# Attention and a two-layer block on one Trainium2 core: the first three batches in an order written as one list, V of the first batch transposed on TensorE

## The chip, the cores and the metric

The kernel runs on one core of one Trainium2 chip. A core has five engines that run beside each other and wait for one another through semaphores: TensorE (PE in the profile; its weight loads are PEld), VectorE (DVE), ScalarE (ACT), GpSimd (POOL) and SyncE (SP). Data moves between the chip's memory (HBM) and the core's SBUF by DMA, issued here by POOL (which can turn float32 into bf16 on the way) and by SP. Results of TensorE go to PSUM, eight banks of 128 x 512 float32. The metric is the device time of one launch in microseconds; several runs give a median.

## What is computed

For 8 batches of 8 heads, 576 positions and head size 64, each query sees itself and the 63 keys before it. The result is laid out as 4608 tokens of 512 features and goes through two matrix products with h - tanh(h) between them.

```python
scores = scale * np.matmul(q, k.transpose(0, 1, 3, 2))
mask = (rel >= 0) & (rel < window)          # rel = query - key, window = 64
attn = softmax(np.where(mask, scores, -1e9))
x = np.matmul(attn, v).transpose(0, 2, 1, 3).reshape(B * S, H * D)
h = x @ w_in                                # 512 -> 2048
out = (h - np.tanh(h)) @ w_out              # 2048 -> 512
```

## The kernel before

**Attention.** A batch is worked on in four pairs of heads; `g` counts the pairs through all batches (0 to 31), so batch 0 is g = 0 to 3, batch 1 is 4 to 7, batch 2 is 8 to 11. Loads put six neighbouring positions of a head in one partition. Q and K are transposed on TensorE (`tr_heads`, `tr_rows`, `tr`: groups of six or twelve small transposes into one PSUM bank) and copied to SBUF in order of position by VectorE or ScalarE (line 85 or 83, the helper `move`). There are nine query blocks of 64; a block meets a window of 128 keys. Scores come out with keys on partitions, ScalarE takes the exponential into `PT`. Keys outside the window are dealt with in one of two ways: "hide" adds a large negative number ahead of the scores by two matmuls per group (`hides`, line 276), "mask" multiplies the exponentials by 0 or 1 on VectorE (line 295). The product with V carries a column of ones, so that sums come with it; `norm` or the end of `tile_pv` takes the reciprocal and multiplies (lines 308, 310, 343).

**V.** V is needed as nine overlapping windows of 128 keys (`vw`). It is loaded eight positions to a partition, cast to `vb` (`cast_v`), sent by DMA to the even windows and one half window (`windows_v`, `keys_v`, line 150 and 165), and the odd windows are copied from the even ones on VectorE (`odd_windows`, lines 454 and 456).

**The two-layer block.** The 4608 tokens are nine chunks of 512. Attention output is transposed on TensorE (`x_tr`, line 349) or by DMA into `xT`. A hidden operation "h" is four 128x512 matmuls (line 383), a tanh on ScalarE (388) and a subtraction on VectorE (395) into `gT`; there are 16 per chunk. An output operation "y" is four matmuls (407); four of them make 128 rows of the output, which ScalarE copies to SBUF (412) and SP sends out.

**Order.** Every engine runs its instructions in the order in which the program writes them; nothing is reordered by a planner. `OPS` puts one "h" or "y" on each slot of a time line, and `at(slot, ...)` hangs attention work and loads on slots; a loop at the end walks the slots. Before the loop stands the first batch, written out, with `warm(n)`: matmuls on zeros. Chunk 0's hidden operations have slots 0 to 30, chunk 1's 32 to 62, chunk 0's outputs 64 to 79. From slot 80 on, hidden operations of chunk c and outputs of chunk c - 1 take turns. Batches 1 and 2 hang on slots 0 to 78. POOL's queue holds, in this order, the loads of batch 0, the window DMAs of batch 0, half of w_in, loads of batch 1, the other half of w_in, and later w_out and batch 3. `pace` makes POOL wait for a subtraction before it issues later loads. POOL has eight DMA semaphores in turn, so a load waits until the one eight before it has landed.

Of the kernel before, what the change touches and what calls it, by code (L numbers as in the profile page):

```python
# [7 lines left out]
F32 = mybir.dt.float32  # L8
# [7 lines left out]
def kernel(  # L16
# [62 lines left out]
    stage, rows, whole = {}, {}, {}  # L79

# [98 lines left out]
    def load_w_in(i):  # L179
        nc.gpsimd.dma_start(out=w_in_sb[i], in_=w_in_r[:, :, 1024 * i:1024 * i + 1024])  # L180
# [39 lines left out]
    nc.vector.memset(vw[0][0:64, 0], 0.0)  # L220
# [13 lines left out]

    def tr_heads(g, which, bank, eng):

        src = stage.pop((g, which))
        tp = ps[:, bank, :].bitcast(BF16)[:, 0:E * P].rearrange("c (e p) -> c e p", e=E)
        for e in range(E):
            for h in range(2):  # L240
                nc.tensor.transpose(tp[64 * h:64 * h + 64, e, :], src[:, h, D * e:D * e + D], ident[:P, :P])
        o = qs[g % 2] if which == "q" else kT[g % NK][:, 64:]
        move(eng, o.rearrange("c (p e) -> c p e", e=E), tp.rearrange("c e p -> c p e"))
# [34 lines left out]

    def tile_scores(g, grp, banks, how="hide"):

        j0, n = GROUPS[grp]
        if how == "hide":
            hides(grp, banks)
        for i in range(n):
            j = j0 + i
            for h in range(2):
                r = slice(64 * h, 64 * h + 64)
                nc.tensor.matmul(ps[:, banks[h], 64 * i:64 * i + 64], kT[g % NK][r, 64 * j:64 * j + 128],  # L288
                                 qs[g % 2][r, 64 * j:64 * j + 64], start=how == "mask", stop=how == "mask" or i == n - 1)
        o = PT[g % NPT][:, j0:j0 + n].rearrange("p j (h t) -> p h j t", h=2)  # L290
        nc.scalar.activation(o, pair_of(banks)[:, :, 0:64 * n].rearrange("p h (j t) -> p h j t", t=64),  # L291
                             ACT.Exp, scale=scale)
        if how == "mask":
            p = PT[g % NPT][:, j0:j0 + n].rearrange("p j (h t) -> p (j h) t", h=2)
            nc.vector.tensor_tensor(p, p, mask_sb.unsqueeze(1).to_broadcast([128, 2 * n, 64]), ALU.mult)

    def tile_pv(g, banks):

        b, pr = divmod(g, NP)
        for i in range(NJ + 1):  # L300
            j = min(i, NJ - 1)
            o = 65 * (i % 5)
            for h in range(2):
                nc.tensor.matmul(ps[64 * h:64 * h + 64, banks[i // 5], o:o + 65], PT[g % NPT][:, j, 64 * h:64 * h + 64],
                                 vw[b % 2][:, j, 2 * pr + h, :], start=True, stop=True)
        ov = pair_of(banks)[:, :, 0:325].rearrange("p n (i c) -> p n i c", c=D + 1)
        rc = sm_pool.tile([128, 2, 5, 1], F32, tag="rc2", name="rc2")
        nc.vector.reciprocal(rc, ov[:, :, :, D:D + 1])
        xo = xs[b % 2].rearrange("p (n i) r d -> p n i r d", i=5)
# [379 lines left out]
```

## Time and profile before

| | |
|---|---|
| median of 3 runs | 334.57 us (332.91 to 336.35) |
| profiled execution | 334.17 us, its span 332.4 us |
| TensorE, VectorE, ScalarE, POOL busy | 315.9, 199.5, 185.1, 110.5 us |
| hidden matmuls (L383) | 576, 146.8 us busy |
| output matmuls (L407) | 560, 140.8 us busy |
| subtraction (L395), tanh (L388) | 144 of 689 ns, 144 of 599 ns |
| mean granted TensorE clock | 0.984 |

"Busy" is the union of the recorded intervals of an engine. Matmuls overlap each other, so one of 379 ns occupies TensorE for about 216 ns when they follow one another (64 output matmuls with what lies between them fill 16.5 us). The page's "chain that ended last" follows the last instruction back to what released it at each step. A wait for several semaphores is put down to the one that came last.

### The profile page before, as it was taken

To read this page: it belongs to the slowest core of one execution; us is meant where nothing else is said; L and a number is where in the kernel's file an instruction comes from. 1 tells how busy PE (TensorE), PEld (TensorE's weight loads), DVE (VectorE), ACT (ScalarE), POOL (GpSimd) and SP (SyncE) were. 2 spreads that over 40 slices of the span, in tenths; PEclk is the share of its full clock that TensorE was granted. 3 is DMA by queue.
4 is the path that set the end of the run, shared out by engine and by line. 5 is a ranking of instruction groups with operands and counts; after the bars stand their busy time and mean duration, and the time that the engine had idled before them with its cause. 6 is when DMAs were issued, how large, how long until landed. Compare 5 with 4: busy or idle time off the path is not lost.

```text
span 332.4 us, 6239 instructions
## 1 busy us (share of the span) xinstructions
PE 315.9 (95%) x2435; PEld 175.3 (53%) x2435; DVE 199.5 (60%) x342; ACT 185.1 (56%) x339; POOL 110.5 (33%) x163
## 2 busy tenths in 40 slices
PE   6868999899999999999999999999999999999995
PEld 2544565555555655555555555555554444444444
DVE  4578698983257675767676666766665444334400
ACT  3545878872566666656666666555544344444411
POOL 8827597005920845434624493300000000000000
PEclk9599999999999999999999999999999999999999
DMA  8999998993796299384976968978004001000021
GB/s 159 184 173 191 212 161 120 199 190 101 123 198 125 41 163 236 81 118 116 176 133 113 180 142 140 204 126 205 32 34 104 32 34 63 32 34 32 32 97 64
DMA packets 46766, 40.68 MB, mean 122 GB/s; under 512 B 18416, under 2 KB 40048, under 8 KB 46544
## 3 DMA queue, kind: packets, MB, share of 16 engines
q0 software_dynamic: 21344, 20.06, 40.1%
q1 hardware_dynamic: 25184, 19.92, 23.6%
q8 instruction: 19, 0.31, 0.4%
q10 hardware_dynamic: 208, 0.29, 0.3%
q14 instruction: 11, 0.09, 0.1%
HBM read 36.70 MB, written 10.62 MB: 142 GB/s over the span
## 4 chain that ended last, share of the span: by engine, by line
PE 71%; DMA 9%; POOL 7%; DVE 7%; ACT 3%; issue 2%; POOLq 0%; DVEq 0%; ACTq 0%
PE ps L407 34%; PE ps L383 27%; DMA wi<-in_moe_w_in_dram 4%; PE ps L332 3%; DMA kall<-in_k_dram 3%; PE ps L316 3%; DVE xs L343 2%; PE ps L249 2%; DMA vw<-vb 2%; DVE qt L85 2%; POOL qall L96 1%; DVE gT L395 1%; POOL kall L96 1%; POOL vall L143 1%; POOL vb L85 1%
## 5 line engine op out<-in xcount | busy, mean ns | idle before, releaser
L383 PE MATMUL ps<-xT,wi 128*128 128x512 bf16 x576 | 146.8, 379 | 2.9 <-DVE gT L395 1.2
L407 PE MATMUL ps<-w_out_sb,gT 128*128 128x512 bf16 x560 | 140.8, 379 | 0.3 <-ACT ysb L412 0.3
L395 DVE TENSOR_TENSOR gT<-ps,th 128x512 bf16<-128x512 f32 x144 | 98.5, 689 | 68.6 <-ACT th L388 67.2
L388 ACT ACTIVATE th<-ps 128x512 f32<-128x512 f32 x144 | 86.0, 599 | 80.8 <-PE ps L383 77.0
L383 PEld LDWEIGHTS <-wi 128*128 128x128 bf16 x576 | 60.5, 113 | 48.1 <-issue 3.0
L407 PEld LDWEIGHTS <-gT 128*128 128x128 bf16 x560 | 52.2, 98 | 53.0 <-issue 0.8
L318 ACT ACTIVATE pt<-ps 128x384 bf16<-128x384 f32 x66 | 32.3, 489 | 24.1 <-PE ps L316 24.1
L85 POOL COPY vb<-vall 72x1024 bf16<-72x1024 bf16 x24 | 24.7, 1052 | 32.6 <-DMA vall<-in_v_dram 29.8
L343 DVE TENSOR_TENSOR xs<-ps,rc 64x576 bf16<-64x576 f32 x44 | 33.2, 755 | 1.1
L412 ACT ACTIVATE ysb<-ps 128x512 f32<-128x512 f32 x35 | 21.0, 599 | 18.9 <-PE ps L407 18.8
L85 DVE COPY qt<-ps 64x576 bf16<-64x576 bf16 x18 | 13.7, 760 | 24.1 <-ACT qt L83 24.1
L85 POOL COPY qb<-qall 96x768 bf16<-96x768 bf16 x20 | 16.6, 830 | 24.6 <-DVE pt L322 16.4
L332 PEld LDWEIGHTS <-pt 128*128 128x128 bf16 x198 | 16.5, 98 | 15.3 <-DVE pt L322 0.8
L332 PE MATMUL ps<-vw,pt 128*128 128x130 bf16 x198 | 22.0, 220 | 0.4 <-DVE pt L322 0.4
L316 PE MATMUL ps<-qt,kt 128*128 128x128 bf16 x198 | 21.8, 219 | 0.0
L316 PEld LDWEIGHTS <-kt 128*128 128x128 bf16 x198 | 15.4, 98 | 8.9 <-issue 0.3
L85 POOL COPY kb<-kall 96x768 bf16<-96x768 bf16 x20 | 16.6, 828 | 3.0 <-DMA kall<-in_k_dram 3.0
L322 DVE TENSOR_TENSOR pt<-pt,ps 128x1152 bf16<-128x1152 bf16 x22 | 16.4, 745 | 0.8 <-ACT pt L318 0.8
L83 ACT ACTIVATE kt<-ps 128x576 bf16<-128x576 bf16 x22 | 14.4, 654 | 1.6 <-PE ps L249 1.5
L291 ACT ACTIVATE pt<-ps 128x640 bf16<-128x640 f32 (+1 forms) x20 | 12.5, 648 | 2.9 <-PE ps L288 2.9
L96 POOL DMA_DIRECT2D qall<-in_q_dram x15 | 9.9, 662 | 7.9 <-DMA wi<-in_moe_w_in_dram 7.0
L83 ACT ACTIVATE qt<-ps 64x576 bf16<-64x576 bf16 x18 | 11.5, 638 | 1.0 <-PE ps L249 0.9
(79 smaller groups left out, 205.1 us busy)
## 6 DMA issues: line engine op xcount, KB each, us to landing
out_dram<-ysb SPq DMA_DIRECT2D x35, 256.0 KB
vall<-in_v_dram POOLq DMA_DIRECT2D x5, 576.0 KB, 10.7
qall<-in_q_dram POOLq DMA_DIRECT2D x4, 576.0 KB, 11.6
kall<-in_k_dram POOLq DMA_DIRECT2D x4, 576.0 KB, 11.5
kall<-in_k_dram POOLq DMA_DIRECT2D x15, 144.0 KB, 5.4
qall<-in_q_dram POOLq DMA_DIRECT2D x15, 144.0 KB, 5.2
wi<-in_moe_w_in_dram POOLq DMA_DIRECT2D x2, 1024.0 KB, 11.3
w_out_sb<-in_moe_w_out_dram POOLq DMA_DIRECT2D x2, 1024.0 KB, 14.3
```

The lines of the kernel that those rows point to most:

```text
L83: nc.scalar.activation(o, i, ACT.Copy)
L85: eng.tensor_copy(o, i)
L96: eng.dma_start(out=t, in_=(q if n == "q" else k)[b, pr::NP].rearrange("h (p e) d -> p h (e d)", e=E))
L316: nc.tensor.matmul(sp[:, i, :], kT[g % NK][:, 64 * j:64 * j + 128], qT[g % NR][:, :, 64 * j:64 * j + 64], start=True, stop=True)
L318: nc.scalar.activation(PT[g % NPT][:, 3 * grp:3 * grp + 3, :], sp, ACT.Exp, scale=scale)
L332: nc.tensor.matmul(ps[:, 5 + grp, 130 * i:130 * i + 130], PT[g % NPT][:, j, :], vw[b % 2][:, j, 2 * pr:2 * pr + 2, :], start=True, stop=True)
L343: nc.vector.tensor_tensor(xo[r, :, :, pr, :], ov[r, :, :, h, 0:D], rc[r].to_broadcast([64, 3, 3, 64]), ALU.mult)
L383: nc.tensor.matmul(hp, w_in_tile(ki, m), chunk_tile(c)[:, :, ki % 2, 64 * (ki // 2):64 * (ki // 2) + 64], start=(ki == 0), stop=(ki == 3))
L388: nc.scalar.activation(th, hp, ACT.Tanh)
L395: nc.vector.tensor_tensor(gT[c][:, m, :], hp, th, ALU.subtract)
L407: nc.tensor.matmul(yp, gT[c][:, m, s * 128:(s + 1) * 128], w_out_sb[:, m, :], start=(m == 0), stop=(m == M - 1))
L412: nc.scalar.activation(ysb, ps[:, yp_bank(c, s), :], ACT.Copy)
```

## The change

The order of everything up to slot 80 is now one list, `FIRST`. Each entry is an operation, its pair or chunk, and where it matters the engine: T is a transposing group of q, k or v and C the copy that follows it; H, S, E and M are hide, scores, exponential and mask of the first five (a) or last four (b) query blocks; W transposes V back and X copies it into the windows; PV and N are the product with V and the normalisation; Y and Z transpose x and copy it; h, t and u are hidden matmuls, tanh and subtraction; y and yo are outputs; kc, qc and Vc are casts; mv is the window DMAs and next loads of a batch; od is the odd windows. `BANKS` gives each its PSUM bank, two banks of a pair always next to each other.

Batch 0's V is loaded like q and k (six positions to a partition), transposed on TensorE into `vT` (in order of position), and transposed back in windows of 128 keys, from which copies fill all nine windows: no window DMA and no odd-window copy for batch 0. Its scratch space is the second `gT` buffer. Both weights are loaded straight after batch 0, ahead of batch 1. Chunk 0's 16 hidden operations come first, then its outputs with the attention of batch 1, then chunk 1's hidden operations with batch 2. Hides are used for pairs 0 to 3 and 7, masks for the other pairs up to 11. The `warm` calls after the first nine matmuls are gone. Slots from 80 on are as before, but for a step or two of batch 3, one turn of x, and a fourth output buffer.

```diff
+    scratch = g_pool.tile([128, M, TOK], BF16, tag="gT", name="scratch").rearrange("p m t -> p (m t)")
+    v0 = scratch[0:P, 0:H * E * D].rearrange("p (h c) -> p h c", h=H)
+    vT = scratch[:, H * E * D:H * E * D + NP * (64 + S)].rearrange("p (i c) -> p i c", i=NP)
...
+    def load_v0(pr):
+        nc.gpsimd.dma_start(out=v0[:, pr::NP], in_=v[0, pr::NP].rearrange("h (p e) d -> p h (e d)", e=E))
+        stage[pr, "v"] = v0[:, pr::NP]
...
-    for pr in range(NP):
-        load_v(0, pr)
+    load_v0(0)
     make_ident()
     load(1, "k", G)
     load(1, "q", G)
     make_hide()
+    load_v0(1)
+    load(2, "k", G)
+    load(2, "q", G)
+    load_v0(2)
+    load_v0(3)
+    load(3, "k", G)
+    load(3, "q", G)
     make_seen()
...
+    load_w_in(0, 0, 512)
+    load_w_in(0, 512, 1024)
+    load_w_in(1)
+    load_w_out(0)
+    load_w_out(1)
+    for pr in range(NP):
+        load_v(1, pr)
+    for g in 4, 5:
+        load(g, "k", G)
+        load(g, "q", G)
...
+    FIRST = """
+        Ha.0 Ha.1 qc.0.D Tq.0 kc.0.A Tv.0 Tk.0 Tk.1 Cq.0.D Tq.1 Cv.0.A Ck.0.D Wb.0 Cq.1.D Sa.0 Ck.1.A Ea.0 Tv.1
+        Sa.1 Hb.0 Ea.1 Wa.0 Xb.0.D Sb.0 Cv.1.D Wb.1 Xa.0.D Tk.2 Eb.0 Xb.1.D Ck.2.A Tq.2 PV.0 N.0 Hb.1 Cq.2.A
+        Wa.1 Sb.1 Tv.2 Eb.1 Tv.3 Hb.2 Sb.2 Xa.1.D Cv.3.D Ha.2 Sa.2 Cv.2.A Eb.2 Tk.3 Tq.3 Wa.2 Ea.2 Wb.2 Ck.3.D
+        Cq.3.A Wb.3 Wa.3 Xa.2.D Xb.2.A Ha.3 Sa.3 Ea.3 Xb.3.D Xa.3.D PV.2 Hb.3 Sb.3 PV.1 Eb.3 N.2 N.1 PV.3 Yb.0.0
+        Zb.0.0.A N.3 Ya.0.0 Ya.0.1 Za.0.0.D Yb.0.1 Za.0.1.A Zb.0.1.D h.0.0 h.0.1 h.0.2 t.0.0 t.0.1 u.0.0 h.0.3
+        h.0.4 t.0.2 h.0.5 t.0.3 h.0.6 u.0.1 u.0.2 u.0.3 t.0.4 h.0.7 t.0.5 u.0.4 h.0.8 h.0.9 t.0.6 u.0.5 t.0.7
+        u.0.6 h.0.10 u.0.7 t.0.8 t.0.9 u.0.8 h.0.11 t.0.10 u.0.9 t.0.11 u.0.10 u.0.11 h.0.12 t.0.12 h.0.13
+        u.0.12 t.0.13 h.0.14 u.0.13 t.0.14 h.0.15 Vc.4.A y.0 t.0.15 u.0.14 Vc.6.A y.1 u.0.15 kc.4.D Vc.7.D y.2
+        y.3 qc.4.D Vc.5.A y.4 mv.1 yo.0 kc.5.D Tk.4 Tq.4 y.5 Ck.4.A Tk.5 qc.5.A Cq.4.D Sa.4 Tq.5 Cq.5.D Ck.5.A
+        Ea.4 y.6 Ma.4 Sb.5 Sb.4 Sa.5 y.7 kc.6.D Eb.5 Eb.4 Mb.5 Ea.5 y.8 qc.6.A od.1 kc.7.A Tk.6 y.9 Tq.6 qc.7.D
+        Ck.6.A Ma.5 Mb.4 y.10 Cq.6.A Tq.7 yo.1 Cq.7.D Tk.7 Sa.6 Sb.6 Ck.7.A y.11 PV.4 Vc.9.D Ea.6 PV.5 y.12
+        Vc.10.D yo.2 y.13 Ma.6 N.4 Eb.6 kc.8.A Mb.6 Hb.7 Ha.7 Tk.8 N.5 Vc.8.D qc.8.D Sa.7 Ck.8.D Sb.7 PV.6
+        Vc.11.A mv.2 Ea.7 Eb.7 N.6 y.14 kc.9.A Yb.1.0 PV.7 qc.9.D Zb.1.0.A Tq.8 Tq.9 y.15 Cq.8.A N.7 Cq.9.D
+        Yb.1.1 yo.3 Ya.1.0 Tk.9 Ya.1.1 Za.1.0.D Sa.8 Zb.1.1.A Ck.9.A Sb.8 Za.1.1.D h.1.0 Ea.8 qc.10.D h.1.1 od.2
+        Sb.9 Eb.8 h.1.2 t.1.0 Eb.9 t.1.1 kc.10.D t.1.2 Mb.8 Tq.10 Ma.8 Sa.9 u.1.0 Cq.10.A PV.8 u.1.1 Ea.9 h.1.3
+        u.1.2 t.1.3 Tk.10 Ck.10.A h.1.4 Mb.9 Ma.9 h.1.5 Sa.10 t.1.4 u.1.3 N.8 kc.11.D PV.9 Ea.10 u.1.4 N.9 h.1.6
+        t.1.5 Tk.11 t.1.6 h.1.7 u.1.5 u.1.6 qc.11.A t.1.7 Ma.10 u.1.7 h.1.8 t.1.8 Ya.2.0 Tq.11 Sb.10 Eb.10 Mb.10
+        Cq.11.A h.1.9 Ck.11.A h.1.10 Za.2.0.D t.1.9 u.1.8 PV.10 t.1.10 N.10 Sb.11 h.1.11 Sa.11 u.1.9 u.1.10
+        Eb.11 Yb.2.0 Ea.11 Mb.11 Ma.11 h.1.12 h.1.13 t.1.11 Zb.2.0.A PV.11 t.1.12 u.1.11 N.11 u.1.12 h.1.14
+        h.1.15 t.1.13 t.1.14 t.1.15 u.1.13 Ya.2.1 Za.2.1.D Yb.2.1 Zb.2.1.A u.1.14 u.1.15
+    """.split()
...
+    def v_tr(c, g):
+        j0, n = half(c)
+        tp = v_psum(c, g)
+        for i in range(n):
+            nc.tensor.transpose(tp[:, i].rearrange("p h d -> p (h d)"), vT[:, g, 64 * (j0 + i):64 * (j0 + i) + 128], ident)
+
+    def v_copy(c, g, eng):
+        j0, n = half(c)
+        move(eng, vw[0][:, j0:j0 + n, 2 * g:2 * g + 2, 0:D], v_psum(c, g))
...
+    def first_moves(b):
+        even_windows(b, G, Y, G, Y, G)
+        if b == 1:
+            for g in 6, 7:
+                load(g, "k", G)
+                load(g, "q", G)
+            for pr in range(NP):
+                load_v(2, pr)
+            for g in 8, 9:
+                load(g, "k", G)
+                load(g, "q", G)
+        else:
+            for g in 10, 11:
+                load(g, "k", G)
+                load(g, "q", G)
...
+    warm(9)
+    for t in FIRST:
+        if t == "y.0":
+            see()
+            copy_mask()
+        first(t)
+    load_all(3, "q")
+    load_all(3, "k")
+    load_v_all(3)
+    at(67, lambda: nc.gpsimd.tensor_copy(tick, gT[1][0:1, 9, 0:1]))
...
-    STEPS = {2: (0, 0, 49, 57), 3: (72, 79, 86, 93), 4: (100, 107, 114, 121), 5: (128, 135, 142, 149)}
-    TURNS = {13: (97, 3, 99, 3), 15: (110, 4, 111, 3)}
+    STEPS = {3: (74, 80, 87, 93), 4: (100, 107, 114, 121), 5: (128, 135, 142, 149)}
+    TURNS = {13: (98, 3, 99, 3), 15: (110, 4, 111, 3)}
```

## The prediction

> **What bounds the kernel now.** I read the page's shares and slices first, then the chain of work that ended last, then a table of stretches.
>
> ```profile
> span 332.4 us, 6239 instructions
> ...
> PE 315.9 (95%) x2435; PEld 175.3 (53%) x2435; DVE 199.5 (60%) x342; ACT 185.1 (56%) x339; POOL 110.5 (33%) x163
> ...
> PE   6868999899999999999999999999999999999995
> ...
> PEclk9599999999999999999999999999999999999999
> ...
> PE 71%; DMA 9%; POOL 7%; DVE 7%; ACT 3%; issue 2%; POOLq 0%; DVEq 0%; ACTq 0%
> ```
>
> TensorE is the bound, with 16.5 us of the span not busy (332.4 - 315.9). The first slices are the weak ones, in activity and in clock. The table of stretches (columns: stretch, length, busy us of PE, PEld, DVE, ACT, POOL with their instructions, clock, DMA share, GB/s) says where:
>
> ```profile
> 0.00:25.10 25.10, 17.49 (x289) 10.52 (x289) 14.97 (x36) 11.41 (x19) 15.98 (x31) 0.80 1.01 172
> 25.10:50.60 25.50, 23.89 (x293) 14.01 (x294) 21.16 (x42) 18.24 (x33) 19.30 (x27) 1.00 1.13 183
> 50.60:73.00 22.40, 20.55 (x220) 12.15 (x218) 20.05 (x40) 19.63 (x38) 5.99 (x10) 1.00 1.05 175
> 73.00:89.49 16.49, 16.49 (x120) 8.94 (x118) 5.98 (x11) 5.99 (x12) 11.34 (x18) 1.00 0.59 113
> ...
> 130.00:332.40 202.40, 197.76 (x1217) 106.53 (x1215) 111.41 (x176) 103.61 (x188) 41.64 (x58) 1.00 0.46 99
> ```
>
> Up to 25.1 us the first batch's attention runs before any chunk exists. Then come 48 us in which hidden matmuls, attention of two batches, tanh and subtractions share the core: TensorE is free for 3.5 us (47.9 - 44.44), but VectorE is busy for 41.2 of them. From 73 us the chunk-0 outputs run with VectorE at 36%. The first hidden matmul of chunk 2, where the two orders meet again, starts at 89.49. All that follows takes 332.4 - 89.5 = 242.9 us. So the change is decided ahead of 89.5 us.
>
> In single microseconds (same columns) the clock:
>
> ```profile
> 8.00:9.00 1.00, 0.99 (x17) 0.37 (x10) 0.68 (x2) 0.70 (x1) 1.00 (x2) 0.50 1.28 187
> ...
> 12.00:13.00 1.00, 1.00 (x30) 0.88 (x30) 0.34 (x1) 0.00 (x0) 0.88 (x3) 0.50 1.06 192
> ...
> 16.00:17.00 1.00, 1.00 (x8) 0.43 (x4) 0.91 (x2) 1.00 (x3) 1.00 (x2) 0.50 0.83 131
> ...
> 19.00:20.00 1.00, 1.00 (x63) 0.99 (x64) 0.45 (x2) 0.00 (x0) 0.00 (x0) 1.00 0.99 147
> ```
>
> It is half from 8.0 to 18.2 us, and TensorE is busy for most of it.
>
> **What the Trainium skill says.** "TensorE: Matmul & The Clock Gate", Part 1: the clock is set by activity windows of 3413 ns. The trace agrees: 18.2 - 8.0 = 10.2 us is three of them. The same page, Part 4: transposes do not count as busy in the way that matmuls do. The trace agrees: from 11.4 to 14.8 us TensorE did 2.1 us of transposes and about 0.7 of matmuls and stayed at half; from 14.8 to 18.2, with 2.9 us of score, hide and warm matmuls, it came up. "VectorE: DVE Perf Modes", Why PSUM operands drop a tier: a PSUM source may still be packed as 16-bit data, no more. Here a contiguous 128x512 copy takes 0.42 us and a strided 128x576 one 0.76: so I bound the new copies with these two.
>
> **The change, part by part.**
>
> *First batch, V on TensorE.* Removed: four value casts on VectorE (4 x 0.43), nine window DMAs and two odd-window copies (0.86 + 0.70). Added: four groups of 12 transposes (L241's: 0.69 us each at half clock, 0.30 at full), four more copies out of PSUM (0.76 on VectorE, 0.65 on ScalarE), 36 transposes back (nine x-transposes take 0.50 at full, so about 1.0 per pair at half), eight copies into the windows. These write 64-element runs; per 576 elements 0.47 (contiguous row) to 0.84 (strided row plus a tenth), taken 0.64. Hides for pairs 1 and 2 replace two masks: +1.12 us each on TensorE at half clock, -0.91 each on VectorE. The sum for TensorE from the first transpose to the last x-transpose at half clock: 12 x 0.69 + 4 x 1.0 + 3 x 1.12 + 4 x 0.66 (scores) + 4 x 0.7 (PV, half-clock value between 0.4 and 0.9, its 80 take 1.65 at full) + 1.0 = 22.1; at full 11.8. Before, the same sum without the 4 groups, the way back and two hides is 13.1. Half clock runs from 8.0 to 18.2. Four groups fit ahead of 8.0; 19.3 half-clock us remain; 9.5 of them are done by 18.2 (pair 1's data lands by then, 0.7 us of waiting); the other 9.8 become 4.9 at full: 23.1, if the clock comes up at 18.2. VectorE's sum here is 14.5 us from 5.2 on and its last items are three normalisations (1.04 each) in a row, then x-copies: the last of them starts behind PV of pair 3 near 23, ends near 24.5, transposes 0.25, copy 0.6. **First hidden matmul at 25.4 us against 25.1.** What the window DMAs cost comes back as TensorE work at half clock.
>
> *Weights first.* The view of waits has the wait that this removes:
>
> ```profile
> POOL qall L96 <- DMA wi<-in_moe_w_in_dram: 7.0, 1, 7.0
> ```
>
> The hidden weights land at 25.07 in the kernel before, so moving them alone gains nothing beyond 25.1. Behind them on POOL's queue now stand w_out (2 x 1024 KB), v of batch 1, then q and k. By GB/s times length the queue moves 4.3 MB by 25.1 and 172-183 GB/s after. Ahead of w_out's end lie 6.3 MB (about 36 us), batch 1's v 6.9 (39), q/k of pairs 4 and 5 7.5 (42). They are wanted at 39 to 44: hidden, with 0 to 1 us to spare; a microsecond late costs one.
>
> *Chunk 0 alone, then its outputs with batch 1.* 16 hidden operations x 4 x 0.216 = 13.8 us; ScalarE 16 x 0.60 and VectorE 16 x 0.69 fit under it. 25.4 + 13.8 = 39.2. Outputs: 16 x 0.864 = 13.8, with six pairs' transposes (0.50), five scores (0.45), one hide (0.7), four PV (0.44), x-transposes (1.0): 22.5 us on TensorE; ScalarE 21.6, VectorE 18.6. The even windows' DMAs and the loads of pairs 6 and 7 are issued only after V's casts, near 43.3; three issues of 0.62 and 4-5 us to landing (5.2-5.4 is the page's median) put k of pair 6 at 49-50, and VectorE, in order, stands at its cast from 47.7. The masks behind it wait, TensorE at pair 6's transposes. I take 1.5 us, between 0 and 3. End: 63.2.
>
> *Chunk 1 with batch 2.* TensorE 18.9 us; VectorE 16 x 0.685 + 4 x 1.04 + 8 masks 3.6 + odd windows 1.4 + copies and casts 1.9 = 22.1: VectorE is the bound. The odd windows wait for DMAs issued after the last cast, near 59.5, and landing near 65.5, where VectorE is ready at 63.8: 1.7 (0 to 3). Subtractions queue behind, tanh's three buffers fill, TensorE stands. Last, pair 12's transposes and first scores stand ahead of chunk 2's first hidden matmul with nothing between: two ScalarE copies behind the last tanh and x-copy, 1.6 us (1 to 3). 63.2 + 22.1 + 1.7 + 1.6 = **88.6 us, against 89.5.** Deferred past this point: a score group and pair 13's q transposes (0.17 + 0.26) and their bubbles, 0.7.
>
> *The rest*: 242.9 + 0.7. The moved turns (97 to 98) and steps cost nothing: hidden and output matmuls on both sides cover them; without that cover 0.3 each. A fourth output buffer: nothing, since the view of waits after 89 us names none on these buffers. On SP's queue the window DMAs of batch 2 now stand behind three outputs of chunk 0, whose evictions are done by 57: nothing, and what the outputs are late if not. Batch 3's loads leave POOL near 62, not 53.7; their 1.8 MB land by 74, and pair 12's first transposes need them at 86: nothing, with 12 us of cover, and microsecond for microsecond beyond. Span 88.6 + 243.6 = 332.2, against 332.4. The profiled execution took 334.17, 1.77 beyond its span; the median shown, 334.57, is 0.4 above that. 332.2 + 1.77 is 333.97; I forecast **334.0**, no change.
>
> **The rivals.**
> *The order fits as written* (faster). For it: VectorE is at 36% from 73 to 89 us, and the new order gives that stretch attention work. TensorE's work from 25 to the meeting point is 13.8 + 22.5 + 18.9 = 55.2 us where the kernel before spends 64.4. If the clock is up earlier (h0 at 23.4, -2.0), the loads arrive in time (-1.5, -1.7) and the end costs 0.6 (-1.0), it is 327.8. Against it: VectorE's 22.1 in the last stretch.
> *The clock stays at half* (slower). Place: the window from 14.8 to 18.2, where the new order has about 2.0 us of real matmuls, not 2.9, among transposes; the warm matmuls at 17.7, 20.4 and 22.2 are gone. If it stays half at 18.2, the next window is nearly all transposes, and first-batch work ends 2.0 us later (27.4 for h0); the wait for normalisation then leaves the window to 28.4 half idle, so hidden matmuls run at 0.43 until 31.9: half of 4.5, 2.2 more. 334.0 + 4.2 = 338.2. It decides if the clock is still 0.5 after 21.6.
> *Batch 1 behind the weights is late* (slower): its v lands at 44, not 39; ScalarE's casts of it stand ahead of chunk 0's last tanh, so subtraction and outputs wait: +5, 339.0. Against: the DMA share of 1.0-1.1 held through 73 us.
>
> **How the numbers follow.** No change 0.43, fits 0.25, half clock 0.22, late loads 0.10. Within 1% (331.2 to 337.9, about what a measurement of this kernel can tell from no change) falls most of the first and a third of the others' nearer ends. Faster by over 1%: 0.22 of the second plus 0.05 of the first; slower: 0.15 + 0.09 + 0.06. The 8-in-10 range runs from 327.8 to 339.5; the likeliest case alone runs from 330.5 to 337.
>
> **What would show it.** First hidden matmul at 25 to 26 us; clock half to 18.2 (or beyond 21.6, the second rival); VectorE over 90% busy in the last stretch ahead of chunk 2, its waits on DMA at a k cast near 48 and at the odd windows near 64; chunk 2's first hidden matmul at 88 to 89; all after it within 1 us of 243. I am wrong if chunk 2 starts by 84, if h0 begins before 24, or if the stretch after 89 changes by over 1 us.

## The result, and the profile after

| | before | after |
|---|---|---|
| median (lowest to highest, runs) | 334.57 us (332.91 to 336.35, 3) | 344.74 us (344.13 to 345.02, 3) |
| profiled execution, its span | 334.17, 332.4 us | 345.02, 343.3 us |
| first hidden matmul | 25.1 us | 23.2 us |
| first hidden matmul of chunk 2 | 89.5 us | 98.7 us |

The changed kernel is slower: the ratio is 1.0299, interval 1.0212 to 1.0387. The forecast was 334.0 us, range 327.8 to 339.5. It was wrong. Ratios here and below leave out executions over 1.5% longer than the shortest of their kernel, so that a ratio need not be the quotient of two medians.

The page of the changed kernel (shares, then TensorE's activity and clock in 40 slices of 8.6 us, then the chain that ended last):

```profile
span 343.3 us, 6496 instructions
...
PE 320.9 (93%) x2554; PEld 178.4 (52%) x2554; DVE 200.2 (58%) x346; ACT 191.7 (56%) x342; POOL 102.9 (30%) x155
...
PE   8879949939979999999999999999999999999996
...
PEclk9999996987989999999999999999999999999999
...
PE 70%; DMA 11%; POOL 6%; DVE 6%; ACT 3%; issue 3%; POOLq 0%; DVEq 0%
```

The span is 10.9 us longer. TensorE is busy for 5.0 of them (320.9 against 315.9) and idle for 5.9 more (22.4 against 16.5). The front, slices 1 and 2, is full in clock in this profile. Two holes have come, slice 6 (43 to 51 us) and slice 9 (69 to 77 us), and the clock dips in or behind each.

The same kernel by the stages that the prediction used (stretch, length, busy us of PE, PEld, DVE, ACT, POOL, clock, DMA share, GB/s):

```profile
0.00:23.19 23.19, 18.28 (x376) 12.39 (x377) 14.57 (x36) 12.24 (x20) 15.03 (x29) 1.00 1.08 184
23.19:37.19 14.00, 14.00 (x68) 7.29 (x66) 10.14 (x16) 9.51 (x17) 1.90 (x3) 1.00 1.12 208
37.19:67.77 30.58, 25.58 (x331) 15.11 (x329) 16.98 (x37) 20.03 (x33) 14.62 (x23) 0.89 0.82 133
67.77:98.69 30.92, 23.64 (x261) 13.19 (x256) 21.05 (x41) 19.34 (x36) 9.37 (x14) 0.89 0.58 91
98.69:343.30 244.61, 239.37 (x1534) 130.42 (x1531) 137.44 (x217) 130.62 (x239) 61.95 (x88) 0.99 0.53 106
```

Against the forecast: front 23.2 (25.4), -2.2; chunk 0's hidden operations 14.0 (13.8), +0.2; outputs with batch 1 30.6 (24.0), +6.6; chunk 1 with batch 2 30.9 (25.4), +5.5; the rest 244.6 (243.6), +1.0. That is +11.1, the whole distance between 343.3 and the forecast span of 332.2. Both bad stages have TensorE idle (5.0 and 7.3 us) and a clock of 0.89.

The view of waits of the changed kernel from 25 to 100 us (who waited, for whom: us in total, times, longest):

```profile
POOL tick L653 <- DVE gT L355: 20.9, 1, 20.9
...
POOL vw L173 <- PE ps L541: 7.7, 1, 7.7
DVE kb L93 <- DMA kall<-in_k_dram: 6.6, 1, 6.6
DVE qb L93 <- DMA qall<-in_q_dram: 6.2, 2, 5.7
...
POOL vw L173 <- ACT vb L91: 5.4, 1, 5.4
PE ps L511 <- DVE kb L93: 5.0, 1, 5.0
...
PE ps L511 <- DVE qb L93: 3.3, 1, 3.3
```

It is the same chain twice: POOL waits ahead of the window DMAs (`vw`), a cast on VectorE waits for a load that stands behind them, TensorE waits for the cast ahead of its transposes. (The second wait of POOL is put down to scores, L541; in the list, `mv.2` follows a V cast that is itself behind exponentials on ScalarE.) POOL's own time line shows the first of them (start, length, what, and in brackets the idle time ahead of it):

```profile
40.68 0.61 POOL L173 DMA_DIRECT2D vw<-vb  x1 [5.37 <-ACT vb L91]
41.28 1.06 POOL L158 DMA_DIRECT2D vw<-vb  x2
42.33 0.66 POOL L104 DMA_DIRECT2D kall<-in_k_dram  x1
```

For 5.4 us POOL stands for ScalarE's last V cast, with pair 6's k, which depends on no cast, behind it. That k is issued at 42.33; VectorE gets it at 51.76, 9.4 us later. In stretches of 2 us (columns as above):

```profile
40.00:42.00 2.00, 2.00 (x20) 1.18 (x19) 0.35 (x2) 1.02 (x3) 1.32 (x3) 1.00 0.11 20
42.00:44.00 2.00, 2.00 (x33) 1.27 (x30) 0.76 (x1) 2.00 (x4) 2.00 (x4) 1.00 1.04 107
50.00:52.00 2.00, 0.00 (x0) 0.00 (x0) 0.24 (x1) 0.00 (x0) 0.67 (x1) 0.74 1.21 206
52.00:54.00 2.00, 1.83 (x10) 1.00 (x11) 1.85 (x4) 1.50 (x2) 1.69 (x2) 0.50 0.98 152
...
72.00:74.00 2.00, 0.00 (x0) 0.00 (x0) 0.26 (x1) 0.00 (x0) 0.00 (x0) 1.00 1.26 230
...
76.00:78.00 2.00, 1.27 (x22) 0.92 (x23) 2.00 (x5) 0.00 (x0) 0.00 (x0) 0.50 1.31 203
```

The DMA engines are all but idle up to 42 (share 0.11), while POOL stands; then all at once they have more than they can do, at 107 GB/s with the windows among it. TensorE is idle from 47 to 52 and from 71 to 74, and with each hole comes a spell of half clock of 6.8 us, from 51.0 to 57.8 and from 74.8 to 81.7. In the second, q of pair 10 is issued at 65.44 behind the windows of batch 2 and used at 73.74.

### The profile page after: what moved, and what is told of

The parts are those of the page before. It is cut to its first block, busy times and chain, and to the rows that moved or that the text cites. A ratio compares the mean times of both kernels' runs of the same rounds, so it can differ in the third digit from the quotient of the medians.

```text
span 343.3 us, 6496 instructions
## 1 busy us (share of the span) xinstructions
PE 320.9 (93%) x2554; PEld 178.4 (52%) x2554; DVE 200.2 (58%) x346; ACT 191.7 (56%) x342; POOL 102.9 (30%) x155
## 4 chain that ended last, share of the span: by engine, by line
PE 70%; DMA 11%; POOL 6%; DVE 6%; ACT 3%; issue 3%; POOLq 0%; DVEq 0%
PE ps L338 30%; PE ps L367 29%; DMA vall<-in_v_dram 5%; DMA kall<-in_k_dram 3%; DMA qall<-in_q_dram 2%; PE ps L288 2%; DVE xs L299 2%; PE ps L276 2%; POOL vb L93 2%; DMA scratch<-in_v_dram 1%; POOL vw L158 1%; PE ps L251 1%; PE ps L563 1%; DVE qt L93 1%; PE ps L382 1%
## 5 line engine op out<-in xcount | busy, mean ns | idle before, releaser
L367 PE MATMUL ps<-w_out_sb,gT 128*128 128x512 bf16 x560 | 143.2, 384 | 0.0
L278 ACT ACTIVATE pt<-ps 128x384 bf16<-128x384 f32 x60 | 29.3, 488 | 21.2 <-PE ps L276 21.1
L299 DVE TENSOR_TENSOR xs<-ps,rc 64x576 bf16<-64x576 f32 x40 | 30.2, 755 | 1.0
L93 POOL COPY vb<-vall 72x1024 bf16<-72x1024 bf16 x20 | 20.7, 1051 | 31.5 <-DMA vall<-in_v_dram 17.5
L93 DVE COPY qt<-ps 64x576 bf16<-64x576 bf16 x16 | 12.2, 760 | 22.3 <-ACT qt L91 22.3
L288 PEld LDWEIGHTS <-pt 128*128 128x128 bf16 x180 | 15.1, 98 | 13.8
L276 PE MATMUL ps<-qt,kt 128*128 128x128 bf16 x180 | 19.8, 219 | 0.9 <-DVE qt L93 0.9
L288 PE MATMUL ps<-vw,pt 128*128 128x130 bf16 x180 | 20.1, 220 | 0.0
L546 ACT ACTIVATE pt<-ps 128x640 bf16<-128x640 f32 (+1 forms) x24 | 15.2, 654 | 5.5 <-PE ps L541 5.1
L91 ACT ACTIVATE kt<-ps 128x576 bf16<-128x576 bf16 x25 | 16.3, 650 | 2.4 <-PE ps L511 2.1
L282 DVE TENSOR_TENSOR pt<-pt,ps 128x1152 bf16<-128x1152 bf16 x20 | 14.9, 743 | 0.0
L104 POOL DMA_DIRECT2D kall<-in_k_dram x15 | 9.9, 663 | 7.2 <-DMA w_out_sb<-in_moe_w_out_dram 4.3
```

What stands on the lines that cost most here:

```text
L91: nc.scalar.activation(o, i, ACT.Copy)
L93: eng.tensor_copy(o, i)
L104: eng.dma_start(out=t, in_=(q if n == "q" else k)[b, pr::NP].rearrange("h (p e) d -> p h (e d)", e=E))
L276: nc.tensor.matmul(sp[:, i, :], kT[g % NK][:, 64 * j:64 * j + 128], qT[g % NR][:, :, 64 * j:64 * j + 64], start=True, stop=True)
L278: nc.scalar.activation(PT[g % NPT][:, 3 * grp:3 * grp + 3, :], sp, ACT.Exp, scale=scale)
L288: nc.tensor.matmul(ps[:, 5 + grp, 130 * i:130 * i + 130], PT[g % NPT][:, j, :], vw[b % 2][:, j, 2 * pr:2 * pr + 2, :], start=True, stop=True)
```

## The experiments

The theory: **the place in POOL's queue.** Loads 6, 7, 10 and 11 are late because they stand behind window DMAs that wait for V's casts, and each hole then costs a spell of half clock on top. The first rival: **bandwidth.** The weights ahead of batch 1 fill the DMA engines, and the loads would be late from any place. The second: the whole order costs more than the old one, whatever its loads do.

**The loads ahead of the windows**

```diff
     def first_moves(b):
+        for g in (6, 7) if b == 1 else (10, 11):
+            load(g, "k", G)
+            load(g, "q", G)
         even_windows(b, G, Y, G, Y, G)
         if b == 1:
-            for g in 6, 7:
...
-        else:
-            for g in 10, 11:
```

> Edit: POOL issues the q and k loads of pairs 6, 7 (and of 10, 11) ahead of the window DMAs of their batch, not behind them. Queue theory: the loads stand behind window DMAs that wait for the last V cast, the DMA engines idle from 40 to 42 us meanwhile, and VectorE and TensorE then wait 5.0 and 3.3 us for k of pair 6 and q of pair 10 and drop to half clock after it. Then both stalls go with their half clock, about 4.5 + 2.5 + 3 + 2.5: 331 to 334 us, first hidden matmul of chunk 2 near 87 to 90. Bandwidth rival (weights first push everything behind them back, so that the DMA engines are simply full): the loads land no earlier, 343 to 346 us.

335.69 us (333.78 to 338.93, 7 runs), ratio 1.0033 [0.9995, 1.0072]: 9 us of the loss of 10.2 are gone by moving eight loads. Its stages 3, 4 and 5, from a profile of the longest of the seven executions (338.93 us):

```profile
38.12:64.56 26.44, 24.41 (x331) 14.41 (x329) 16.96 (x37) 19.68 (x33) 14.63 (x23) 0.94 1.06 173
64.56:89.18 24.62, 21.20 (x262) 12.59 (x257) 20.51 (x41) 19.24 (x36) 7.45 (x11) 1.00 0.58 90
89.18:337.20 248.02, 239.60 (x1534) 130.85 (x1531) 138.06 (x217) 130.96 (x239) 62.28 (x88) 0.99 0.53 105
```

Chunk 2 starts at 89.2, where the forecast had 88.6, and stages 3 and 4 take 26.4 and 24.6 where it had 24.0 and 25.4. So the order is as good as forecast, and bandwidth is not what holds it: the same bytes move. But the rest takes 248.0; its reason is looked for further down.

**The holes filled with matmuls on zeros**

```diff
     for t in FIRST:
+        if t == "Tk.6":
+            warm(20, 3)
+        if t == "Tq.10":
+            warm(14, 7)
```

> Edit: 20 matmuls on zeros ahead of pair 6's k transposes and 14 ahead of pair 10's q transposes, in the two gaps where TensorE waits; everything else as in the changed kernel. Theory that half clock after a gap is a cost of its own: clock 1.0 through both stretches, gaps as before, 339 to 341 us. If the half clock is hidden under the waits of other engines: 343 to 346 us.

340.87 us (339.66 to 342.32, 4 runs), ratio 1.0201 [1.0159, 1.0242]. Here the loads come as late as in the changed kernel, and TensorE does useless work while it waits. Stages 3 and 4:

```profile
36.96:64.25 27.29, 27.24 (x351) 15.62 (x349) 16.96 (x37) 19.90 (x33) 14.65 (x24) 1.00 0.94 152
64.25:92.77 28.52, 24.41 (x276) 13.98 (x270) 20.59 (x41) 19.35 (x36) 9.53 (x14) 0.99 0.63 99
```

The clock is 1.00 and 0.99 instead of 0.89 twice. So 3.9 of the 10.2 us (344.74 - 340.87) are the half clock behind the holes, and not the holes. Between the two profiled spans it is 5.3 us (343.3 and 338.0). Had the prediction known their length, it would still have missed this.

**w_out behind batch 1's values and pairs 4 and 5**

```diff
     load_w_in(1)
-    load_w_out(0)
-    load_w_out(1)
...
         load(g, "q", G)
+    load_w_out(0)
+    load_w_out(1)
```

> Edit: w_out is loaded behind batch 1's v and the q, k of pairs 4 and 5, not ahead of them; w_in stays first. Queue theory: batch 1's casts were not late, the gap at pair 6 stays; w_out lands near 42 and chunk 0's outputs wait for it at 37: 345 to 350 us. Bandwidth rival: the first loads of batch 1 land 10 us earlier and the stretch of batch 1 gets shorter, 335 to 342 us.

343.28 us (342.9 to 343.8, 4 runs), ratio 1.0271 [1.0234, 1.0308]: 1.5 us less than the changed kernel, and a miss of both theories. POOL's time line:

```profile
41.74 0.62 POOL L173 DMA_DIRECT2D vw<-vb  x1 [12.15 <-ACT vb L91]
```

Batch 1's values are in early, but their casts stand behind chunk 0's tanhs on ScalarE as before, and POOL now stands 12.2 us for them. K of pair 6, issued at 43.40, is used at 52.17, against 51.76 in the changed kernel. TensorE's wait there is shorter (1.7 against 5.0 us) since the outputs have already waited 2.5 us for w_out, and the hole at q of pair 10 stays at 3.5. Values that land early gain little while POOL waits for their casts. On bandwidth this run says nothing: `w_out`, for which TensorE waits until 42.6 here, still stands ahead of that load on POOL's queue.

**The loads first, but as late as before.** This parts the issue time from the place in the queue: a small GpSimd copy makes the loads of pairs 6 and 7 wait for the cast for which the windows waited. Those of pairs 10 and 11 stay where they were, and so does the second hole.

```diff
+        if b == 1:
+            nc.gpsimd.tensor_copy(tick, vb[0:1, 0, 2, 0:1])
+            for g in 6, 7:
+                load(g, "k", G)
+                load(g, "q", G)
         even_windows(b, G, Y, G, Y, G)
```

> The changed kernel, with the loads of pairs 6 and 7 ahead of batch 1's window transfers, but behind a GpSimd copy that waits for the same last V cast on ScalarE: the loads go out at the same time as the windows did, 40.7, no earlier. Rival first: if the position behind the window transfers in the queue is what made them late, they land 2 us after issue at 44 to 46, the gap at pair 6 is under 1 us and the time 338 to 340.5. If the late issue (GpSimd stands 5.4 us for ScalarE's cast) is what counts, they land at 46 to 48, 3 us of the gap stay and the time is 342 to 344.

343.16 us (342.51 to 343.32, 4 runs), ratio 1.0234 [1.018, 1.0289]. It takes both to explain. VectorE's time line in this kernel:

```profile
45.73 0.35 DVE L93 COPY kb<-kall 96x768 bf16<-96x768 bf16 x1
...
52.19 0.70 DVE L413 COPY vw<-vw 64x2080 bf16<-64x2080 bf16 x1 [5.33 <-DMA vw<-vb]
```

Issued at 41.3 and ahead of the windows, k of pair 6 is there by 45.7, 4.4 us later instead of 9.4: the place alone is worth 5 us for that load. But the windows, issued 3 us later than in the changed kernel, are now what VectorE waits for, at the odd-window copies, which start at 52.19, against 52.48 in the changed kernel. Pair 7's q cast is behind them, and TensorE stands 4.0 us. One of the two is late as long as both leave POOL after 40.7; in the first experiment the loads left from 36.2 on, while POOL would have stood idle. **What counts for batch 1 is that the loads leave while POOL would else stand and the DMA engines are all but idle; reordering what leaves after that changed mainly which of VectorE's steps waits.**

**The rest: the tick, and one step of batch 3.** In the experiment with the loads ahead, POOL's longest single wait, and the wait of TensorE for POOL's casts behind it, from 85 to 125 us:

```profile
POOL tick L649 <- DVE gT L355: 17.3, 1, 17.3
...
PE ps L251 <- POOL qb L93: 3.0, 2, 2.2
```

The changed kernel has a copy on POOL (`at(67, ...)`, L653 there; L649 here) that waits for chunk 1's tenth subtraction; batch 3's casts and batch 4's loads stand behind it. TensorE's 2.2 us, up to 116.6, are followed by half clock from 117.3 to 120.7. Without the copy (and with the loads ahead):

```diff
-    at(67, lambda: nc.gpsimd.tensor_copy(tick, gT[1][0:1, 9, 0:1]))
```

> Edit: as e1_loads_ahead, and POOL no longer waits for chunk 1's tenth subtraction (slot 67) before it casts batch 3. Theory that this wait holds batch 3 back once the stretch ahead is shorter (POOL stood 17.3 us there in e1, then batch 4's v was issued at 93.6 and landed at 111.8, and TensorE waited 2.2 us at 116.6): POOL's casts start near 72 to 75, the part after chunk 2's first hidden matmul falls from 248 back to 243 to 245: 330 to 333 us. If POOL's casts beside the last stretch slow VectorE, or batch 4's v does not come earlier: 335 to 338 us.

Ratio 0.9904 [0.9876, 0.9933] (median 334.35 of 20 runs, 329.16 to 339.56). The last stage of its profile:

```profile
86.84:330.40 243.56, 239.03 (x1533) 130.63 (x1531) 137.51 (x217) 130.51 (x239) 58.90 (x83) 0.99 0.54 105
```

TensorE's wait for POOL is gone, and the rest falls from 248.0 to 243.6, the forecast's own figure. But the 248.0 is from the longest of seven executions, and the ratio rests on the 8 shortest of 20. By the medians of all runs, each against the kernel before beside it (335.69 and 334.33; 334.35 and 334.86), leaving out the tick gains 1.9 us, and this kernel is no faster than the kernel before. And with batch 3's first step one slot later besides:

```diff
-    STEPS = {3: (74, 80, 87, 93), 4: (100, 107, 114, 121), 5: (128, 135, 142, 149)}
+    STEPS = {3: (75, 80, 87, 93), 4: (100, 107, 114, 121), 5: (128, 135, 142, 149)}
```

> Edit: as e5_no_tick, and the steps of pair 12 hang one slot later (75 instead of 74), so that chunk 2's first hidden matmul stands ahead of pair 12's first scores. Theory that the tail before chunk 2 is a wait of TensorE for the copies of pair 12 alone (1.0 us of it named so): 1 to 2 us less than e5. If the hidden matmul itself is held by the last x copies: the same as e5 within 0.5 us.

331.79 us (331.38 to 332.25, 4 runs), ratio 0.99 [0.9865, 0.9934]: 1% faster than the kernel before. The 12 runs of this kernel and of the two below that are built on it lie between 329.0 and 333.2. What the step is worth by itself isn't shown, since why the kernel without it spreads over 10 us isn't known. Stages 3 to 5:

```profile
37.78:62.73 24.95, 22.94 (x331) 13.79 (x329) 16.92 (x37) 19.69 (x33) 14.43 (x23) 1.00 1.11 182
62.73:86.33 23.60, 20.89 (x257) 12.34 (x254) 19.74 (x40) 18.40 (x35) 9.12 (x13) 1.00 0.70 104
86.33:329.90 243.57, 238.28 (x1538) 130.28 (x1534) 138.26 (x218) 130.95 (x241) 60.42 (x86) 1.00 0.53 106
```

The clock is full in all three. The second rival of the experiments has fallen: the new order, fed in time, is the shorter one, by about 1%.

**What is left of the holes.** In that kernel VectorE still stands up to 3.2 us at the odd windows and TensorE 2.0 us behind it. Two more edits on top of it:

```diff
-        Ea.4 y.6 Ma.4 Sb.5 Sb.4 Sa.5 y.7 kc.6.D Eb.5 Eb.4 Mb.5 Ea.5 y.8 qc.6.A od.1 kc.7.A Tk.6 y.9 Tq.6 qc.7.D
-        Ck.6.A Ma.5 Mb.4 y.10 Cq.6.A Tq.7 yo.1 Cq.7.D Tk.7 Sa.6 Sb.6 Ck.7.A y.11 PV.4 Vc.9.D Ea.6 PV.5 y.12
+        Ea.4 y.6 Ma.4 Sb.5 Sb.4 Sa.5 y.7 kc.6.D Eb.5 Eb.4 Mb.5 Ea.5 y.8 qc.6.A kc.7.A Tk.6 y.9 Tq.6 qc.7.D
+        Ck.6.A Ma.5 Mb.4 od.1 y.10 Cq.6.A Tq.7 yo.1 Cq.7.D Tk.7 Sa.6 Sb.6 Ck.7.A y.11 PV.4 Vc.9.D Ea.6 PV.5 y.12
...
-        Yb.1.1 yo.3 Ya.1.0 Tk.9 Ya.1.1 Za.1.0.D Sa.8 Zb.1.1.A Ck.9.A Sb.8 Za.1.1.D h.1.0 Ea.8 qc.10.D h.1.1 od.2
-        Sb.9 Eb.8 h.1.2 t.1.0 Eb.9 t.1.1 kc.10.D t.1.2 Mb.8 Tq.10 Ma.8 Sa.9 u.1.0 Cq.10.A PV.8 u.1.1 Ea.9 h.1.3
+        Yb.1.1 yo.3 Ya.1.0 Tk.9 Ya.1.1 Za.1.0.D Sa.8 Zb.1.1.A Ck.9.A Sb.8 Za.1.1.D h.1.0 Ea.8 qc.10.D h.1.1
+        Sb.9 Eb.8 h.1.2 t.1.0 Eb.9 t.1.1 kc.10.D t.1.2 Mb.8 Tq.10 Ma.8 od.2 Sa.9 u.1.0 Cq.10.A PV.8 u.1.1 Ea.9 h.1.3
```

> The changed kernel with loads 6, 7, 10, 11 ahead of the windows, without the tick at step 67, first step of batch 3 at 75, and besides with VectorE's copies from the odd windows moved back: batch 1's behind pair 7's query cast and the masks of pairs 5 and 4, batch 2's behind pair 8's second mask. Theory (VectorE standing 3.16 us at those copies is what leaves TensorE 1.95 us idle at pair 7's transposes): that gap goes under 0.8 us, chunk 2 starts at 84.5 to 85.6 instead of 86.3, 329.5 to 331.2 us. Rival (the copies are short of nothing but their windows, and PV of batch 1 then waits for them in their new place): the gap only moves, 331.5 to 333.

330.85 us (329.0 to 332.71, 4 runs), ratio 0.9871 [0.9798, 0.9943]. The four runs span what both sides expected. By the profile the rival is right: chunk 2 starts at 87.1 and not at 84.5 to 85.6, and TensorE's longest wait is now

```profile
PE ps L563 <- DVE vw L415: 2.1, 1, 2.1
```

at the product with V of pair 8, which needs those very copies. The hole has moved, and this kernel can't be told from the one without the edit. Then pair 12's transposes in other banks:

```diff
-            at(a, tr, g, "q", 2 if g < 13 else 3, A, V)
-            at(a + 2, tr, g, "k", 3, A)
+            at(a, tr, g, "q", 5 if g < 13 else 3, A, V)
+            at(a + 2, tr, g, "k", 1 if g < 13 else 3, A)
```

> The kernel with the odd windows' copies moved back, and besides pair 12's transposes into banks 5 and 1 instead of 2 and 3. Theory (the 1.0 us before chunk 2 comes from chunk 1's last subtractions alone, which hold the banks): the wait stays if it is the hidden matmuls' own (they wait for gT), so no more than 0.5 us, 329 to 331 us. Rival (pair 12's transposes wait behind the banks and hold TensorE's queue): 1 us or more less than without.

331.84 us (330.99 to 333.18, 4 runs), ratio 0.9892 [0.9827, 0.9957]. The waits at L251 that it aims at (1.2 us in all) are gone from the view, so they were waits for the banks, but the wait for the odd windows at pair 8 is 3.4 us here instead of 2.1, and the time is the same.

**Parts of the change, apart.** The kernel before, with both weights moved to just behind batch 0's windows, and nothing else:

```diff
     load_w_in(0)
+    load_w_in(1)
+    load_w_out(0)
+    load_w_out(1)
     for pr in range(NP):
         load_v(1, pr)
...
-    load_w_in(1)
...
-    at(23, load_w_out, 0)
-    at(23, load_w_out, 1)
```

> Edit: the kernel before with both weights loaded straight after batch 0's window DMAs, ahead of batch 1; its order of work is kept. Theory that weights first costs only where attention of batch 1 is wanted early: batch 1's q and k land near 40 instead of 30 to 38, its steps among chunk 0's hidden operations stand, 340 to 346 us. If the loads have slack there: 333 to 336 us.

347.9 us (347.26 to 349.95, 4 runs), ratio 1.0391 [1.0343, 1.0438]. Batch 1's values are late: VectorE stands 14.7 us at a cast, subtractions are behind it, hidden matmuls stop for 13.7. The old order mixes chunk 0 with batch 1, so the weights alone, put first, cost it 13 us; its first hidden matmul is at 24.0. The other part the other way round: the changed kernel, with batch 0's V cast and cut into windows by DMA, on SP.

```diff
-    load_v0(0)
+    load_v(0, 0)
...
-        elif n in ("Ck", "Cq", "Cv"):
+        elif n == "Cv":
+            cast_v(0, a[0], eng)
+        elif n in ("Ck", "Cq"):
...
+    FIRST = [t for t in FIRST if t[:2] not in ("Tv", "Wa", "Wb", "Xa", "Xb") and t not in ("PV.0", "N.0")]
+    i = FIRST.index("PV.2")
+    FIRST[i:i] = ["od.0", "PV.0", "N.0"]
+    FIRST.insert(FIRST.index("Cv.2.A") + 1, "w0.0")
+    FIRST_OPS["w0"] = lambda _: even_windows(0, Y, Y, Y, Y, Y)
```

> The changed kernel, but batch 0's V is taken the old way: V is cast and the windows are cut by transfers from SBUF to SBUF, with copies for the odd ones; the two sets of transposes of V and their copies are left out; everything behind the first hidden matmul as in the changed kernel. If V on TensorE is what brought the first hidden matmul from 25.1 to 23.2: it comes at 25 or later here, with TensorE at half clock in front, 345.5 to 349 us. If it gains nothing by itself: first hidden matmul at 22 to 23.5, 343.5 to 345 us.

360.99 us (358.91 to 362.56, 4 runs), ratio 1.0766 [1.0696, 1.0836], far beyond what either side expected; the first hidden matmul comes at 40.9, behind half clock from 12.0 on. TensorE's waits of this kernel:

```profile
PE ps L563 <- DVE vw L415: 11.3, 1, 11.3
PE ps L563 <- DMA vw<-vb: 4.1, 1, 4.1
```

and its DMA queues from 14.8 to 32 us (packets, megabytes, the time of the packets as a share of 16 engines):

```profile
q0 software_dynamic: 1708, 3.25, 100.4%
q1 hardware_dynamic: 648, 0.60, 13.0%
```

Five window DMAs of 0.6 MB in all leave SP between 14.9 and 18.2, beside 3.2 MB of weights and loads, and the odd-window copies that need them start at 31.9. So in the changed kernel V on TensorE is worth 16 us (360.99 - 344.74) against windows that are issued into the weights. Against windows ahead of the weights it wasn't tried, nor in the old order alone; in the kernel just above, the windows stood ahead of the weights on POOL's queue, and the front was no later than 24.0.

**What keeps the clock up in front.** Half clock from 8.0 to 18.2 was the prediction's first step, and the profile after shows none. Leaving out the hides of pairs 1 and 2 in the changed kernel:

```diff
-    HIDE = (0, 1, 2, 3, 7)
+    HIDE = (0, 3, 7)
...
+        if t in ("Ha.1", "Hb.1", "Ha.2", "Hb.2"):
+            continue
```

> Edit: the hides of pairs 1 and 2 are left out, and nothing takes their place, so keys outside the window count in these two pairs: it shows what eight plain matmuls in the first batch do to the clock and the time. Theory that hides keep the clock at full there: TensorE at 0.5 from 8 to 18 us as in the kernel before, first hidden matmul near 25 to 27 us. If the clock was up for another reason: clock 1.0, first hidden matmul at 22.5 to 23.2.

345.06 us (one run); the clock is 1.00 up to the first hidden matmul at 22.0, with TensorE busy for 16.9 us of 22. So it isn't the hides of these two pairs. Then the kernel before, with 13 warm matmuls in place of 9:

```diff
-    warm(9)
+    warm(13)
```

> Edit: the kernel before with 13 instead of 9 warm matmuls on zeros at the start, which fill TensorE's gap from 5.15 to 6.3 us and nothing else. Theory that the gaps from 4.6 to 8.0 us (TensorE busy about 45 per cent) turned the clock to half from 8 to 18 us, and that filling them is what kept it at full in the changed kernel: clock 1.0 from 8 us on, the first hidden matmul still near 25 because its weights land at 25.07: 332.5 to 334.5 us. If hides and transposes of the changed order kept it up: half clock as before, 334 to 335 us.

335.42 us (333.18 to 337.9, 12 runs), ratio 1.002 [0.9992, 1.0048], not the 332.5 to 334.5 expected. The clock holds past 8 us and falls at 13.6, after the next idle place (TensorE 1.61 us busy from 11 to 14). Last, both idle places filled, once with `idle_tr(n)`, n transposes of the identity into a bank that nobody reads, once with matmuls on zeros:

```diff
     warm(9)
+    idle_tr(18)
...
+    idle_tr(24)
     tr_heads(2, "k", 2, V)
```

> The kernel before, with transposes of the identity into a bank that nobody reads, in the two places where TensorE stands in front: 18 behind the nine warm matmuls, 24 ahead of pair 2's transposes (which wait for their load). Theory A (any work of TensorE keeps the clock up, transposes too): full clock to 17 us at least, and half for less than 4 us in front. Theory B (transposes do not count, as the prediction assumed): clock half from about 8, as in the kernel before, 334 to 337 us. Under A the time is 333 to 335.5, since the weights land at 24 to 25 in any case.

334.84 us (332.92 to 336.95, 20 runs), ratio 1.0008 [0.9986, 1.003]. Stretches of its front; the first line is the same stretch of the kernel before:

```profile
5.00:8.00 3.00, 1.45 (x37) 0.97 (x36) 1.74 (x4) 1.49 (x2) 2.86 (x8) 0.99 1.23 184
...
5.00:8.00 3.00, 2.87 (x46) 2.09 (x44) 1.32 (x3) 1.31 (x2) 2.86 (x8) 1.00 1.24 193
...
11.00:14.00 3.00, 2.17 (x62) 1.81 (x61) 1.37 (x3) 1.52 (x4) 2.50 (x4) 1.00 1.13 201
14.00:16.00 2.00, 1.24 (x43) 1.01 (x44) 1.52 (x3) 1.58 (x3) 0.86 (x2) 1.00 0.92 216
16.00:19.00 3.00, 1.76 (x26) 1.12 (x26) 1.61 (x4) 1.84 (x3) 2.49 (x4) 0.54 1.09 184
```

```diff
-    warm(9)
+    warm(13)
...
+    warm(7)
     tr_heads(2, "k", 2, V)
```

> The same two places filled with matmuls on zeros instead: 13 in front, 7 more ahead of pair 2's transposes. Both theories: full clock to 17 us at least; first hidden matmul at 23.5 to 24.5, 333 to 335.5 us. Only if the clock still falls near 14, as it did with the first place alone filled, is it something else than TensorE's idle time that brings it down.

335.0 us (332.38 to 337.1, 12 runs), ratio 1.0019 [0.9989, 1.0049]. The same stretches of this kernel, where the two differ most:

```profile
11.00:14.00 3.00, 2.63 (x59) 1.62 (x58) 1.29 (x3) 1.35 (x4) 2.64 (x5) 1.00 1.18 227
...
16.00:19.00 3.00, 1.85 (x70) 1.48 (x71) 2.35 (x5) 1.80 (x4) 2.33 (x4) 1.00 1.10 198
```

With transposes the clock stays full past 8 and past 14 and falls only at 16.2, after 3 us in which TensorE twice waited for a load; it is half until 23.0, for longer than the 4 us expected. **Transposes keep a full clock up**, as matmuls do. The Trainium skill ("TensorE: Matmul & The Clock Gate", Part 4) has it that the full clock doesn't engage for transposes, since they don't count as busy in the same way; for holding a clock that is already full these runs say otherwise. With matmuls it never falls, the first hidden matmul comes at 23.4 instead of 25.1, and the profiled span is 330.6 instead of 332.4; yet that profile is of the shortest of the 12 runs, and their median is no better than before.

Transposes count for raising the clock, too. The kernel with pair 12's transposes in other banks keeps the changed kernel's order in front, and its profile has a spell of half clock there. Here are the stretch ahead of the spell, the spell, and the spell for L581 alone, the transposes of x:

```profile
17.48:20.90 3.42, 1.85 (x66) 1.34 (x65) 2.13 (x5) 1.30 (x2) 0.85 (x2) 1.00 1.14 213
20.90:24.31 3.41, 3.05 (x26) 2.37 (x26) 1.81 (x5) 1.36 (x3) 0.00 (x0) 0.50 1.11 216
...
20.90:24.31 3.41, 2.29 (x18) 0.50 1.11 216
```

Of TensorE's 3.05 us of work in the spell 2.29 were transposes, and at its end the clock was full again. Three other profiles show the same, with 2.06 to 2.28 us of transposes in 3.15 to 3.24 of work. So the prediction read too much into the profile before, where TensorE stayed at half from 11.4 to 14.8 us with 2.1 us of transposes. It was busy for 2.64 us there, and with 13 warm matmuls it stayed at half through 2.67 us in 3.42 (from 16.96) without a single transpose.

One profile of a front is also only one case of it. Of the eight other runs that keep the changed kernel's order in front, six have a spell of half clock of 3.4 us between 11.5 and 25.2 us, and two have none; their first hidden matmul comes at 21.9 to 24.0. The kernel before, in the 31 executions taken beside the last two experiments, has a mean clock of 0.974 to 1.0; the profile that the prediction rests on has 0.984. The 11 of them at 0.995 or more have a median of 334.38 us, the other 20 of 334.70. So a full clock goes with some 0.3 us less in that kernel, which fits with filling its idle places gaining nothing that these runs can tell. With transposes the lowest mean clock of 20 runs is 0.985, with matmuls of 12 runs 0.985.

## Why the prediction was wrong

*Front* (25.4, measured 23.2). Wrong to the good side. The step was "half clock runs from 8.0 to 18.2", taken over from the profile before. There the clock fell after a stretch with 1.45 us of work in 3 (5 to 8 us); the new order has 2.9 there, of hides and of transposes, V's among them, which the prediction had set down as not counting. The added TensorE work was counted at half clock and ran at full, or nearly so: at most 3.4 us of half clock stand in front in the other runs of this order. The profile before was one case of a clock that changes from one execution to the next.

*Chunk 0 alone* (13.8, measured 14.0): right. *The rest* (243.6, measured 244.6): 1.0 us more, with a third spell of half clock in it, 3.4 us from 98.7, behind a stretch of 3.42 us in which TensorE worked for 1.30; at full clock throughout, the mended kernel (loads ahead, no tick, the step at 75) takes 243.57. The tick at slot 67 wasn't priced. What it costs here isn't shown; in the kernel with the loads ahead it is 1.9 us by the medians and 4.4 by two profiles (248.0 against 243.6).

*Outputs with batch 1* (22.5 + 1.5). This is **the step that failed**: the wait for the loads of pair 6, put at 1.5 us, and the half clock behind it, put at nothing. The mechanism was named: loads 6 and 7 behind windows behind V's casts, VectorE in order at pair 6's k, TensorE at its transposes. Its sizes were not: k usable at 51.8, not 49 to 50 (9.4 us from issue to use, where the page before has a median of 5.2 to 5.4 to landing); VectorE at its cast at 45.2, not 47.7, since the faster front brings everything forward except what waits for POOL; a wait of 6.6 us, not 1.5. So the gain in front came to nothing here.

*The price of a hole* was left out: the stall was put in as its own length. TensorE ran at half clock from 51.0 to 57.8 us, with 5.6 us of work, so by estimate 2.8 us more. The Trainium skill's page "TensorE: Matmul & The Clock Gate", in "Why this matters for your kernels", has the rule that applies: no idle gaps of TensorE over about 3 us between bursts of matmuls, or it goes back to half rate. The trace agrees at the 5.0 us hole, and at the second, of 3.3 us with one of 1.9 close behind, which brought half clock from 74.8 to 81.7 us, with 4.9 us of work. The second experiment, which filled both holes, was 3.9 us faster.

*Chunk 1 with batch 2* (22.1 + 1.7 + 1.6). VectorE's sum was near (21.05 us busy, forecast 22.1), but TensorE's was not: 20.9 us at full clock in the mended kernel, forecast 18.9, more than VectorE's 19.7 there. So VectorE as the bound isn't shown. And the stop came one place earlier than forecast, at q of pair 10 and not at the odd windows behind it, and again with 8.3 us from issue to use. With the loads in time, this stage took 24.6 and the stop was the odd windows, as forecast.

*Rivals.* "The order fits as written" (327.8) was right in kind for the mended kernels, which take 330.85 to 331.84, between it and the forecast's 334.0, but not for this kernel. "The clock stays half in front" and "batch 1 behind the weights" had the right sign for other reasons. None had the loads' wait as the slower case, because the forecast itself had it, with 3 us as its end; the range's upper end of 339.5 took in no half clock behind it.

## What to carry to other kernels

A transfer's time starts when its queue comes to it: before pricing a landing, walk the issuing engine's list and ask what each entry ahead waits for; a load that needs nothing must not stand behind one that waits for a cast. An idle hole of TensorE is dearer than its length, since the clock falls and the work behind it runs at half, here for 3.4 or 6.8 us. A clock read from one profile is one case: before building on it, look at the mean clock of other executions. What a part of a change is worth depends on what stands around it (16 us here, against windows that meet the weights), so try its removal from the new kernel as well as its addition to the old.

## What the runs showed of the hardware

- Transposes put into TensorE's idle places hold the full clock, and a spell of half clock with 2.29 us of transposes in 3.05 of work ended in full clock. In these profiles the spells last 3.4 us or a multiple of it (3.4, 6.8 and 10.2 in those shown). With each profile cut into such stretches from the times at which its clock changed, half clock followed every full-clock stretch with at most 1.5 us of TensorE's work, and none with 1.97 or more. In between both are found: 1.85 us (17.48 to 20.90, shown above) was followed by half clock, 1.86 in the changed kernel (20.23 to 23.64) was not.
- In the changed kernel a window DMA of 130 KB from SBUF to SBUF took 6.5 us from issue to landing (median of those on POOL, 38 to 76 us), and loads of 144 KB beside them 7.9 to 8.8 (medians of k, q and v); the DMA engines were fully busy then, at 107 GB/s from 42 to 44 us, where from 72 to 74 they moved 230.
- Small transfers on SP's queue beside 1 MB loads on POOL's: of five issued from 14.9 to 18.2, the first that TensorE waited for was in by 21.8, those that VectorE waited for only by 31.9; 13% of the engines' time against 100.4%.
